# First LayerNorm's last eight tiles in two groups of four, transposed by TensorE, one mean-root product per group, and a new order of the whole program

## The chip, the core and the metric

The kernel runs on one core of one Trainium2 chip. Its time is device microseconds (us) of one execution, as the runs measure it; the profile is one such execution with every engine's instructions recorded. The engines are TensorE (PE in the profile; PEld is its weight load), VectorE (DVE), ScalarE (ACT), GpSimd (POOL) and SyncE (SP), which issues nearly all DMAs.

## What is computed

One transformer block on x of 2048 tokens by 512 features in bfloat16, with scales and shifts from a condition vector c:

```python
mod = (silu(c) @ w_mod).reshape(1, 6, 1, -1)           # sa, ca, ga, sb, cb, gb
h = layernorm(x) * (1 + ca) + sa
x = x + ga * A(h)                                      # linear attention
h = layernorm(x) * (1 + cb) + sb
x = x + gb * B(h)                                      # gated MLP, 512 -> 1376 -> 512

def A(h):                                              # 32 heads of 16
    q, k, v = split(h @ wqkv)
    phi(y) = [softmax(y @ w_phi), softmax(-y @ w_phi)] # 32 features a head
    num = phi(q) @ (phi(k)^T v);  den = phi(q) . sum(phi(k))
    return (num / den) @ wo

def B(h):
    return (sigmoid(h @ w_gate) * (h @ w_up)) @ w_down
```

## The kernel before

The 2048 tokens are 16 tiles of 128. The work is cut into some 900 named tasks; each is an instruction or a few on one engine. A text, ORDER, lists all their names in one sequence, written out by hand; `@A`, `@D` and `@P` after a name put it on ScalarE, VectorE or GpSimd where the task allows it, otherwise the first engine that it allows takes it. Each engine runs its own tasks strictly in that sequence, and so does the sync queue. Buffers (8 PSUM banks, 7 two-kilobyte slots for exponentials and features, and so on) are given out along the same sequence. Nothing is decided at run time.

The stages, each with the names used below:

- **Start.** Loads `ld_...`. TensorE transposes the key weight (`tpw`), ScalarE copies it (`wTc`), TensorE multiplies it by the block-diagonal w_phi (`fold`, whose operand `bd` GpSimd builds), ScalarE copies the result (`foldc`). `modc1` are one-column products that turn c into the first norm's scale and shift. `warm` are products on a zero tile whose results nobody reads.
- **First LayerNorm**, in the groups of tiles that LG lists. Per tile: statistics on VectorE (`st1`, lines 702 and 703). Per group: reciprocal root `rs1` (ScalarE by two activations, or GpSimd by two instructions, lines 712 and 713) and, on VectorE, minus mean times root (`nmr1`, line 718). Per tile: normalised tile `xn1` (line 731 on GpSimd). Then the transpose: by TensorE into a PSUM bank (`tph`, line 744; one task per group and 128 features), or, where TD is 1, by a transposing DMA on the sync queue (`xT1`, line 736). Then the scale and shift on the way to h1T (`hm1`, lines 751 and 753: the eviction of the transposes, or, after a DMA, a pass over h1T).
- **Keys and values**, per tile: products `K` (817) and `V` (821), exponentials `e` (776, ScalarE), sums `n` (780, VectorE), reciprocals `r`, features `phi` (787, GpSimd or VectorE), values with a column of ones `va`, and the accumulation `kv` (282) into two banks over all 16 tiles. Then `kvn` and `kvz` copy the sum (294, 299).
- **Queries**, per tile: `Q` (871), `qe`, `qn`, `qphi` (784) and a transposing DMA `pT`. Queries need only h1T, so their place in the order is free up to the use.
- **Attention output**, per tile, once the kv sum is there: numerators `num` (326), reciprocals `rd` (329), division `u` (333), a transpose (`tpo` and `oT` 347 for tiles 0 and 1, a DMA for the others), `out` (356), residual sum `x1` (361).
- **Second LayerNorm**: `st2`, `rs2`, `nmr2` (383), `xn2`, transpose `xnT`, modulation `mod` (422, 424, 426), for tile 0, tile 1, and then pairs.
- **MLP**, in six chunks of 1, 1, 2, 4, 4 and 4 tiles: gate and up products `g` and `u` (447, and 449 and 452 for the last 96 columns), `tg` (457), `hm` (468), and per tile the down products `y` (485), the final sum `fin` (492) and the store `st`. `tsw`, a table load on ScalarE (387), must stand between the last root taken there and the first `tg`. `wd` and `wo` scale the down and output weights.

Of the kernel before, what the change touches and what calls it, by code (L numbers as in the profile page):

```python
# [15 lines left out]
P = 128  # L16
# [14 lines left out]
LG = [[0], [1], [2, 3], [4, 5], [6, 7], [8, 9], [10, 11], [12, 13], [14, 15]]  # L31
TD = [0, 0, 0, 0, 0, 0, 1, 1, 0]
# [7 lines left out]
pmem ld_x0b wdz warm0 c1 warm1_0 warm1_1 bd st1_2 st1_3 warm1_2 warm1_3 c2 rs1_2 ld_x0a ld_wk0 warm1_4 tpw0 st1_0 rs1_0 wTc0 st1_1 ld_wk1 rs1_1 c3 xn1_0  # L40
nmr1_1 nmr1_2 ld_x1b st1_6 st1_7 tpw1 tpw3 wTc3 wTc1 tpw2 fold10 foldc10 wTc2 ld_wm00b ld_x1a ld_wm00a tph00 fold11 fold13 rs1_4 foldc13 fold12 foldc12 xn1_3
xn1_2 xn1_1 modc1.0 tph10 tph11 st1_4 tph20 tph01 ld_x2b foldc11 tph22 warm1_5 modc1c0 hm1_11@A nmr1_4 xn1_6 xn1_7 st1_5 rs1_3@P st1_11 st1_10 warm1_6
hm1_20@A hm1_10@A tph21 warm1_7 tph41 tph42 hm1_21 rs1_6@P nmr1_3 tph13 ld_wm01a ld_wm01b modc1.1 hm1_01@A hm1_00@A hm1_41@A tph03 tph23 K2a ld_x2a tph02
modc1c1 st1_8 ld_x3a warm1_8 K1a hm1_23 xn1_5 xn1_4 tph12 nmr1_6 st1_9 hm1_03@A hm1_13@A hm1_02@A ld_wv0 wqT3 xn1_10 xn1_11 rs1_5@P K0a K0b tph31 hm1_42@A
warm1_9 hm1_12@A hm1_22@A tph32 e0.0 K3a tph30 K3b hm1_30@A ld_wmga K1b tph33 warm1_10 tph40 st1_14 st1_15 st1_13 hm1_31@A hm1_32 wqT0 e3.0 wqT1 K2b hm1_40
nmr1_5 rs1_8@P n0.0 nmr1_8 hm1_33 e2.0 V0a V1a fold03 xn1_9 xn1_8 V1b V0b e1.0 n2.0 V2a V2b tph50 hm1_50 warm1_11 xn1_15 xn1_14 n1.0 V3a wqT2 fold00 fold01
tph43 r0.0@A va1 va0 phi0.0 foldc03 fold02 foldc01 foldc02 n3.0 st1_12 foldc00 xT1_10 xT1_11 r2.0 va2@D ld_wmm2 modca.0 modca.1 hm1_60@P hm1_63@P hm1_62@P
# [113 lines left out]
def kernel(  # L161
# [143 lines left out]
    def downstream(G):  # L305
# [7 lines left out]
        for p, tiles in enumerate(UNITS):  # L313
# [66 lines left out]
            if on_act:  # L380
                def f_nm(e, tiles=tiles):
                    for t in tiles:
                        dve.tensor_scalar(nmr[:, 1, t:t + 1], mv2[:, t, 0:1], rs2[:, t:t + 1], -1.0, op0=ALU.mult, op1=ALU.mult)
                G.add(f"nmr2_{p}", {"DVE": 0.07 * nt}, f_nm,
                      r=[("rs2", p)], w=[("nmr2", p)])
# [673 lines left out]
```

## Time and profile before

| what | us |
|---|---|
| median of 3 runs (lowest, highest) | 205.52 (204.65, 206.97) |
| the profiled execution's own time | 205.02 |
| its span, first to last instruction | 203.3 |
| TensorE busy | 194.9 (96%) |
| VectorE busy | 160.6 (79%) |
| ScalarE busy | 105.9 (52%) |
| GpSimd busy | 102.1 (50%) |
| DMA | 22.94 MB, mean 113 GB/s |

The granted TensorE clock was 1.0 over the span. Times on the trace count from the span's start; the 1.7 us between the span and the execution's own time lie around it. The ends of pipelined products are modelled, so a row's duration for TensorE is not what a product costs in a row of them: that is the distance from start to start. A few records of products are missing from the trace, which shows as a hole of exactly one product's length.

### The profile page before, as it was taken

What the parts mean: (1) busy time and instruction counts of PE and PEld (TensorE: products, weight loads), DVE (VectorE), ACT (ScalarE), POOL (GpSimd) and SP (SyncE); (2) the same over time, 40 slices, a digit from 0 to 9 for tenths busy, and PEclk for the clock granted to TensorE, in tenths of its full rate; (3) what the DMA queues carried; (4) which work ended last, traced back from release to release, by engine and by line L of the source; (5) the groups of instructions that cost most, each with busy time, mean ns of one, the idle gap of its engine ahead of it and who ended that gap; (6) DMA issues with size and microseconds to landing.
All of it is one profiled execution on the core that took longest, in us unless ns stands there. A gap on an engine that the chain in (4) does not pass through costs nothing.

```text
span 203.3 us, 4138 instructions
## 1 busy us (share of the span) xinstructions
PE 194.9 (96%) x1447; PEld 106.7 (52%) x1471; DVE 160.6 (79%) x374; ACT 105.9 (52%) x257; POOL 102.1 (50%) x143
## 2 busy tenths in 40 slices
PE   7789999999999999999999999999999999999993
PEld 2455655555464687668844444444444444444442
DVE  3899999999999999999897797794969844326633
ACT  2799999999978984556451115212113311324100
POOL 4698977789689999767670056230030324000000
PEclk9999999999999999999999999999999999999999
DMA  5999975669952792417637224433112030100111
GB/s 172 331 329 182 233 264 102 123 82 280 400 213 43 146 102 55 94 37 106 125 59 103 51 54 103 101 83 77 26 26 69 13 79 31 40 13 7 50 55 55
DMA packets 49453, 22.94 MB, mean 113 GB/s; under 512 B 38065, under 2 KB 47634, under 8 KB 49426
## 3 DMA queue, kind: packets, MB, share of 16 engines
q1 hardware_dynamic: 48896, 22.59, 48.6%
q8 instruction: 13, 0.21, 0.4%
q14 instruction: 14, 0.11, 0.2%
q10 hardware_dynamic: 530, 0.02, 0.1%
HBM read 11.58 MB, written 2.10 MB: 67 GB/s over the span
## 4 chain that ended last, share of the span: by engine, by line
PE 75%; DVE 8%; ACT 4%; DMA 4%; issue 4%; POOL 3%; SPq 0%; POOLq 0%; DVEq 0%
PE y_ps L485 19%; PE u_ps L447 18%; PE g_ps L447 17%; PE a_ps L356 5%; DMA wmod_sb<-in_w_mod_dram 4%; PE k_ps L817 3%; PE warm L600 3%; DVE ks L780 3%; PE num L326 2%; POOL phi L787 2%; PE q_ps L871 2%; PE v_ps L821 2%; PE g_ps L449 1%; ACT h1T L751 1%; DVE qks L780 1%
## 5 line engine op out<-in xcount | busy, mean ns | idle before, releaser
L457 ACT ACTIVATE tg<-g_ps 128x512 bf16<-128x512 f32 (+5 forms) x66 | 28.8, 455 | 66.7 <-PE g_ps L447 39.5
L468 DVE SCALAR_TENSOR_TENSOR wmod_sb<-tg,u_ps 128x512 bf16<-128x512 bf16 (+4 forms) x63 | 30.3, 492 | 18.0 <-ACT tg L457 11.3
L485 PE MATMUL y_ps<-wd_sb,wmod_sb 128*128 128x512 bf16 (+4 forms) x180 | 44.2, 366 | 0.2
L447 PEld LDWEIGHTS <-wg_sb 128*128 128x128 bf16 (+1 forms) x252 | 21.9, 99 | 16.1 <-issue 0.2
L447 PEld LDWEIGHTS <-wu_sb 128*128 128x128 bf16 (+1 forms) x252 | 21.8, 99 | 16.0 <-issue 0.3
L784 POOL TENSOR_TENSOR qphi<-qe,qks 128x512 bf16<-128x512 bf16 x24 | 25.1, 1063 | 3.9 <-DMA pT<-qphi 1.0
L485 PEld LDWEIGHTS <-wmod_sb 128*128 128x128 bf16 (+1 forms) x187 | 17.1, 98 | 16.0 <-issue 0.6
L447 PE MATMUL u_ps<-wT_sb,wu_sb 128*128 128x512 bf16 (+2 forms) x124 | 23.8, 322 | 0.1
L447 PE MATMUL g_ps<-wT_sb,wg_sb 128*128 128x512 bf16 (+2 forms) x122 | 23.0, 321 | 0.2
L447 PE MATMUL g_ps<-wqk_sb,wg_sb 128*128 128x128 bf16 (+4 forms) x127 | 19.9, 286 | 0.1
L447 PE MATMUL u_ps<-wqk_sb,wu_sb 128*128 128x128 bf16 (+4 forms) x127 | 19.8, 286 | 0.2
L492 DVE TENSOR_TENSOR ot<-y_ps,x 128x512 bf16<-128x512 f32 (+2 forms) x17 | 11.1, 654 | 10.5 <-PE y_ps L485 10.4
L780 DVE TENSOR_REDUCE qks<-qe 128x64 bf16<-128x1024 bf16 x16 | 19.2, 1204 | 0.0
L780 DVE TENSOR_REDUCE ks<-e 128x64 f32<-128x1024 bf16 (+2 forms) x22 | 19.1, 905 | 0.0
L376 POOL TENSOR_SCALAR ve<-mv 128x2 f32<-128x2 f32 (+1 forms) x8 | 1.8, 226 | 34.2 <-DVE mv L366 34.1
L776 ACT ACTIVATE e<-k_ps 128x512 bf16<-128x512 f32 (+2 forms) x44 | 17.7, 504 | 0.1
L776 ACT ACTIVATE qe<-q_ps 128x512 bf16<-128x512 f32 x32 | 17.3, 608 | 0.8 <-POOL phi L787 0.4
L787 POOL TENSOR_TENSOR phi<-e,kr 128x1024 bf16<-128x1024 bf16 (+2 forms) x10 | 14.5, 1454 | 3.9 <-ACT kr L795 2.1
L817 PE MATMUL k_ps<-wqk_f,h1T 128*128 128x512 bf16 x61 | 15.9, 379 | 0.1
L356 PE MATMUL a_ps<-wo_sb,oT 128*128 128x512 bf16 x60 | 15.9, 379 | 0.2
L871 PE MATMUL q_ps<-wqk_f,h1T 128*128 128x512 bf16 x60 | 15.7, 379 | 0.2
L821 PE MATMUL v_ps<-wv_sb,h1T 128*128 128x512 bf16 x62 | 15.5, 379 | 0.0
(131 smaller groups left out, 306.4 us busy)
## 6 DMA issues: line engine op xcount, KB each, us to landing
out_dram<-ot SPq DMA_DIRECT2D x15, 128.0 KB, 1.8
x_sb<-in_A_x_dram SPq DMA_DIRECT2D x6, 256.0 KB, 4.9
wmod_sb<-in_w_mod_dram SPq DMA_DIRECT2D x1, 1536.0 KB, 7.4
wu_sb<-in_B_w_up_dram SPq DMA_DIRECT2D x1, 1376.0 KB, 11.0
wg_sb<-in_B_w_gate_dram SPq DMA_DIRECT2D x1, 1376.0 KB, 10.4
wd_sb<-in_B_w_down_dram SPq DMA_DIRECT2D x1, 1280.0 KB, 8.0
wmod_sb<-in_w_mod_dram SPq DMA_DIRECT2D x4, 256.0 KB, 6.0
wqk_sb<-in_A_wqkv_dram SPq DMA_DIRECT2D x2, 256.0 KB, 4.5
```

Of the source, the lines that this page charges most:

```text
L356: pe.matmul(ap_[:], lhsT=oT[:, j, :], rhs=wo_sb[:, j, :], start=(j == 0), stop=(j == KT - 1))
L447: pe.matmul(ps[:fsz, 0:n], lhsT=w[:, j, ft * P:ft * P + fsz], rhs=h[:, j, 0:n], start=(j == 0), stop=(j == KT - 1))
L457: G.add(f"tg{k}.{ft}", {"ACT": 0.13 + n * 0.00083}, lambda e, tg=tg, g_ps=g_ps, fsz=fsz, n=n: act.activation(tg[:fsz, 0:n], g_ps[:fsz, 0:n ...
L468: dve.scalar_tensor_tensor(hm_all[:fsz, hm[k].slot, ft, 0:n], tg[:fsz, 0:n], 1.0, u_ps[:fsz, 0:n], op0=ALU.add, op1=ALU.mult)
L485: mm = pe.matmul(y[:, 0:c1 - c0], lhsT=hm_all[:fsz, hm[k].slot, ft, tl * P:(tl + 1) * P], rhs=wd_sb[:fsz, ft, c0:c1], start=(ft == 0), sto ...
L776: act.activation(ee[:, a:b, s].rearrange("p g f h -> p g (f h)"), kp[:, a * 64:b * 64].rearrange("p (g n) -> p g n", n=64), ACT.Exp, scale ...
L780: dve.tensor_reduce(ks[:, a:b].rearrange("p g s h -> p (g s) h"), ee[:, a:b].rearrange("p g s f h -> p (g s) h f"), axis=AX.X, op=ALU.add)
L784: engine(e).tensor_tensor(ph[:].rearrange("p (g s f h) -> p g s f h", s=2, f=DH, h=4)[:, :, s], ee[:, :, s], ks[:, :, 1 - s].unsqueeze(2). ...
L787: engine(e).tensor_tensor(ph[:, a * P:b * P].rearrange("p (g f h) -> p g f h", f=DH, h=4), ee[:, a:b].rearrange("p g s f h -> p (g s) f h" ...
L817: pe.matmul(kp[:], lhsT=h1T[:, j, t * P:(t + 1) * P], rhs=wqk_f[:, j, D:2 * D], start=(j == 0), stop=(j == KT - 1))
L821: pe.matmul(vp[:], lhsT=h1T[:, j, t * P:(t + 1) * P], rhs=wv_sb[:, j, :], start=(j == 0), stop=(j == KT - 1))
L871: pe.matmul(qp[:], lhsT=h1T[:, j, t * P:(t + 1) * P], rhs=wqk_f[:, j, 0:D], start=(j == 0), stop=(j == KT - 1))
```

## The change

LG has seven groups instead of nine: tiles 8 to 11 and 12 to 15 are one group each. TD is 0 everywhere, so tiles 10 to 13, which a DMA transposed, are transposed by TensorE too. A group of four fills a bank of 512 columns per 128 features, and one instruction evicts it. Minus mean times root is one instruction per group, in both norms. VectorE may normalise a tile of the first norm. ORDER is new throughout; its rows are not shown here, but as they fall on the engines.

```diff
-LG = [[0], [1], [2, 3], [4, 5], [6, 7], [8, 9], [10, 11], [12, 13], [14, 15]]
-TD = [0, 0, 0, 0, 0, 0, 1, 1, 0]
+LG = [[0], [1], [2, 3], [4, 5], [6, 7], [8, 9, 10, 11], [12, 13, 14, 15]]
+TD = [0, 0, 0, 0, 0, 0, 0]
 ORDER = """
-pmem ld_x0b wdz warm0 c1 warm1_0 warm1_1 bd st1_2 st1_3 warm1_2 warm1_3 c2 rs1_2 ld_x0a ld_wk0 warm1_4 tpw0 st1_0 rs1_0 wTc0 st1_1 ld_wk1 rs1_1 c3 xn1_0
+ld_x0b bd wdz warm0 c1 warm1_0 warm1_1 warm1_2 warm1_3 ld_x1b ld_wk1 ld_x0a c2 st1_3 st1_2 tpw2 tpw3 rs1_2 st1_7 nmr1_2 xn1_2@A wTc2 fold12 xn1_3 ld_wk0 tpw1
...
                 def f_nm(e, tiles=tiles):
-                    for t in tiles:
-                        dve.tensor_scalar(nmr[:, 1, t:t + 1], mv2[:, t, 0:1], rs2[:, t:t + 1], -1.0, op0=ALU.mult, op1=ALU.mult)
-                G.add(f"nmr2_{p}", {"DVE": 0.07 * nt}, f_nm,
+                    a, b = tiles[0], tiles[-1] + 1
+                    dve.scalar_tensor_tensor(nmr[:, 1, a:b], mv2[:, a:b, 0], -1.0, rs2[:, a:b], op0=ALU.mult, op1=ALU.mult)
+                G.add(f"nmr2_{p}", {"DVE": 0.2}, f_nm,
...
             def f_nm(e, ts=ts):
-                for t in ts:
-                    dve.tensor_scalar(nmr[:, 0, t:t + 1], mv1[:, t, 0:1], rs1[:, t:t + 1], -1.0, op0=ALU.mult, op1=ALU.mult)
-            G.add(f"nmr1_{g}", {"DVE": 0.02 + 0.1 * n}, f_nm,
+                a, b = ts[0], ts[-1] + 1
+                dve.scalar_tensor_tensor(nmr[:, 0, a:b], mv1[:, a:b, 0], -1.0, rs1[:, a:b], op0=ALU.mult, op1=ALU.mult)
+            G.add(f"nmr1_{g}", {"DVE": 0.2}, f_nm,
...
-            G.add(f"xn1_{t}", {"POOL": 0.69, "ACT": 0.73} if t else {"DVE": 0.3}, f_xn, ...
+            G.add(f"xn1_{t}", {"POOL": 0.69, "ACT": 0.73, "DVE": 0.4} if t else {"DVE": 0.3}, f_xn, ...
```

How the order falls on the engines at the three places that the prediction speaks of (line numbers after the change are one lower from the list of groups on).

GpSimd at the start, from the block-diagonal operand to the normalised tiles of the groups [2, 3] and [6, 7]. Before:

```order
L580 TENSOR_TENSOR bd_101<-wp_sb_100,bmask_76 128x4x64 x2
L731 TENSOR_SCALAR xn_245<-x_sb_65,rs1_84,nmr_89 128x512
L731 TENSOR_SCALAR xn_247<-x_sb_65,rs1_84,nmr_89 128x512
L731 TENSOR_SCALAR xn_249<-x_sb_65,rs1_84,nmr_89 128x512
L731 TENSOR_SCALAR xn_291<-x_sb_65,rs1_84,nmr_89 128x512
L731 TENSOR_SCALAR xn_293<-x_sb_65,rs1_84,nmr_89 128x512
```

Now, in the same place:

```order
L579 TENSOR_TENSOR bd_101<-wp_sb_100,bmask_76 128x4x64 x2
L730 TENSOR_SCALAR xn_184<-x_sb_65,rs1_84,nmr_89 128x512
L711 TENSOR_SCALAR ve1_83<-mv1_82 128x2
L712 TENSOR_TENSOR rs1_84<-ve1_83,mhalf_79 128x2
L711 TENSOR_SCALAR ve1_83<-mv1_82 128x1
L712 TENSOR_TENSOR rs1_84<-ve1_83,mhalf_79 128x1
L711 TENSOR_SCALAR ve1_83<-mv1_82 128x1
L712 TENSOR_TENSOR rs1_84<-ve1_83,mhalf_79 128x1
L730 TENSOR_SCALAR xn_242<-x_sb_65,rs1_84,nmr_89 128x512
L730 TENSOR_SCALAR xn_244<-x_sb_65,rs1_84,nmr_89 128x512
```

Three root pairs (of the groups [6, 7], [0] and [1]) have come from ScalarE to stand between the first normalised tile and the two of [6, 7]; the tiles 2 and 1 are normalised elsewhere.

VectorE from the copy of the kv sum's last part to the first residual sum (o is the divided output of a tile, den a reciprocal, qks a query sum). Before:

```order
L329 RECIPROCAL den_1233<-num_1208 128x16
L780 TENSOR_REDUCE qks_1240<-qe_1198 128x64
L333 TENSOR_TENSOR o_1242<-num_1183,den_1196 128x256
L329 RECIPROCAL den_1244<-num_1213 128x16
L329 RECIPROCAL den_1271<-num_1235 128x16
L333 TENSOR_TENSOR o_1242<-num_1213,den_1244 128x256
L333 TENSOR_TENSOR o_1231<-num_1235,den_1271 128x256
L361 TENSOR_TENSOR x1_1282<-a_ps_1261,x_sb_65 128x512
```

Now:

```order
L332 TENSOR_TENSOR o_1227<-num_1178,den_1183 128x256
L779 TENSOR_REDUCE qks_1237<-qe_1170 128x64
L332 TENSOR_TENSOR o_1239<-num_1187,den_1218 128x256
L328 RECIPROCAL den_1281<-num_1208 128x16
L360 TENSOR_TENSOR x1_1283<-a_ps_1241,x_sb_65 128x512
```

One division and one reciprocal of tile 1 have moved from ahead of the residual sum to behind it.

ScalarE from the second norm's first root to the modulations of tile 0 (oT is a copied transpose of an attention output). Before:

```order
L347 COPY oT_1304<-tpo_1299 128x512
L373 ACTIVATE ve2_87<-mv2_86,eps_96 128x1
L374 ACTIVATE rs2_88<-ve2_87 128x1
L400 ACTIVATE xn2_1333<-x1_1282,nmr_89,rs2_88 128x512
L387 ACT_TABLE_LOAD
L426 ACTIVATE wqk_sb_98<-tp_x_1344,modc_78 128x128 x2
```

Now:

```order
L372 ACTIVATE ve2_87<-mv2_86,eps_96 128x1
L373 ACTIVATE rs2_88<-ve2_87 128x1
L399 ACTIVATE xn2_1306<-x1_1283,nmr_89,rs2_88 128x512
L386 ACT_TABLE_LOAD
L346 COPY oT_1326<-tpo_1320 128x512
L425 ACTIVATE wqk_sb_98<-tp_x_1311,modc_78 128x128
L425 ACTIVATE wqk_sb_98<-tp_x_1310,modc_78 128x128
```

The copy of tile 1's attention output has moved from ahead of the root to behind the table load.

More of the change, by code (lines that the diff above doesn't have):

```diff
@@ L44 @@
[L44 to L47, printed above, removed]
```

89 lines of the change are left out of this document (46 added, 43 removed).

## The prediction

> **What bounds the kernel now.** I read the windows first, cut at TensorE's first key product, its first numerator product (just after the kv sum) and its first gate product. Columns: stretch, length, then busy time of PE, PEld, DVE, ACT and POOL.
>
> ```profile
> 14.20:58.02 43.82, 43.15 (x393) 24.02 (x397) 42.56 (x84) 42.36 (x117) 35.73 (x41) 1.00 0.90 220
> 58.57:68.89 10.32, 10.21 (x82) 5.52 (x85) 10.18 (x28) 8.67 (x18) 10.16 (x11) 1.00 0.36 73
> 68.89:200.10 131.21, 130.26 (x875) 71.14 (x888) 96.87 (x227) 44.91 (x98) 46.60 (x64) 1.00 0.33 63
> ```
>
> In the first stretch three engines are full at once: TensorE lacks 0.67 us, VectorE 1.3, ScalarE 1.5; only GpSimd has room (8 us). In the last one TensorE is alone at the limit. The idle time before its costliest group, 0.2 us in 174 products, says the same, and the end follows TensorE at a fixed distance:
>
> ```profile
> L485 PE MATMUL y_ps<-wd_sb,wmod_sb 128*128 128x512 bf16 (+4 forms) x174 | 43.9, 371 | 0.2
> 193.80 6.31 PE L485 MATMUL y_ps<-wd_sb,wmod_sb 128*128 128x512 bf16 x38
> 199.52 0.91 DVE L492 TENSOR_TENSOR ot<-y_ps,x 128x384 bf16<-128x384 f32 x2 [0.45 <-PE y_ps L485]
> ```
>
> So from the first gate product at 68.89 on, what counts is how much TensorE work is left when the first gate product starts. Before that it is a race of the engines to that start.
>
> Three spacings are needed:
>
> ```profile
> 62.40 1.02 PE L871 MATMUL q_ps<-wqk_f,h1T 128*128 128x512 bf16 x4
> 60.32 0.39 PE L345 MATMUL tpo<-ident,o 128*128 128x128 bf16 x4
> 28.90 0.82 PE L616 MATMUL modc_ps<-sc_bf,wmod_sb 128*128 128x1 bf16 x24 [0.22 <-DMA wmod_sb<-in_w_mod_dram]
> ```
>
> Four 512-column products take 1.02 us of which the last is 0.38, so they start 0.215 us apart; four transposes take 0.39 with a last one of 0.22, so 0.055 apart. 24 one-column products take 0.82 with a last one of 0.17, so 0.028 apart.
>
> **The change, part by part.**
>
> *Start to first key product.* In the new order GpSimd runs the operands of the folded weight, one normalised tile, three mean-root pairs (all three were ScalarE's) and two more normalised tiles before the transposes that TensorE has ahead of its first key product are fed.
>
> ```profile
> 5.24 1.50 POOL L580 TENSOR_TENSOR bd<-wp_sb,bmask 128x256 bf16<-128x256 bf16 x2 [2.13 <-DMA wp_sb<-in_A_w_phi_dram]
> 12.49 0.23 POOL L712 TENSOR_SCALAR ve<-mv 128x2 f32<-128x2 f32 x1
> 13.52 0.22 POOL L712 TENSOR_SCALAR ve<-mv 128x2 f32<-128x2 f32 x1
> 14.54 3.03 POOL L731 TENSOR_SCALAR xn<-x_sb,rs,nmr 128x512 bf16<-128x512 bf16 x4
> 14.20 0.38 PE L817 MATMUL k_ps<-wqk_f,h1T 128*128 128x512 bf16 x1
> ```
>
> The operands end at 6.74. A mean-root pair takes 13.52 - 12.49 = 1.03, a tile 3.03/4 = 0.76. So GpSimd is through at 6.74 + 0.76 + 3 x 1.03 + 2 x 0.76 = 12.11. TensorE then has nine transposes (0.50), 16 one-column products (0.45) and two hand-overs (about 0.1 each): first key product at about **13.25, 0.95 earlier**. ScalarE loses these three pairs and gains one normalisation, so it isn't later there. Half of the key weight still stands third in the sync queue, so TensorE's first weight transposes start as before.
>
> *First key product to first numerator.* TensorE's sum against before: the query product of tile 13 comes in (4 x 0.215 = +0.86); the first norm's tiles 10 to 13, which a DMA transposed, cost 16 transposes and two more fall behind the first key product (18 x 0.055 = +1.0); four warm-up products leave (-0.86) and two are put at the end, in the gap where the accumulated kv is copied (+0.43, hidden there). Without the hidden two: +1.0. The accumulation ends at 13.25 + 43.82 + 1.0 = **58.07** against 58.02.
>
> Does another engine end later? The rows that price this, grouped by shape (busy time, mean ns of one):
>
> ```profile
> 57.87 0.43 DVE L294 TENSOR_TENSOR kvb<-kvacc,mask 128x256 bf16<-128x256 f32 x1
> L751 ACT ACTIVATE h1T<-tp_h,modc 128x256 bf16<-128x256 bf16 x11 | 6.2, 587 | 0.0
> L753 POOL TENSOR_SCALAR h1T<-h1T,modc 128x256 bf16<-128x256 bf16 x7 | 3.9, 559 | 0.0
> L787 DVE TENSOR_TENSOR phi<-e,kr 128x1024 bf16<-128x1024 bf16 x7 | 4.7, 682 | 0.3 <-POOL h1T L753 0.3
> L787 POOL TENSOR_TENSOR phi<-e,kr 128x1024 bf16<-128x1024 bf16 x5 | 9.6, 1917 | 1.6 <-ACT kr L795 0.9 <-PE kvacc L282 0.5
> L753 DVE TENSOR_SCALAR h1T<-tp_h,modc 128x256 bf16<-128x256 bf16 x9 | 3.5, 393 | 0.6 <-PE tp_h L744 0.6
> L422 DVE TENSOR_SCALAR wqk_sb<-tp_x,modc 128x128 bf16<-128x128 bf16 x2 | 0.6, 340 | 0.0
> L729 DVE TENSOR_SCALAR xn<-x_sb,mv,rs 128x512 bf16<-128x512 bf16 x1 | 0.4, 404 | 0.0
> L718 DVE TENSOR_SCALAR nmr<-mv,rs 128x1 f32<-128x1 f32 x15 | 2.4, 203 | 0.3 <-ACT rs L710 0.3
> L299 DVE SCALAR_TENSOR_TENSOR kvb<-kvacc,mask 128x16 bf16<-128x16 f32 x2 | 0.3, 217 | 0.0
> L361 DVE TENSOR_TENSOR x<-a_ps,x_sb 128x512 f32<-128x512 f32 x16 | 10.8, 682 | 2.0 <-PE a_ps L356 1.8
> ```
>
> I took spacings from the timeline and counted each engine's instructions ahead of the copy of kv. VectorE: 16 evictions of transposes instead of 9, six of them 512 wide (+2.8); six more normalisations (+1.9); six fused mean-root products instead of 15 single ones (-1.0); eight feature products instead of twelve, the whole-tile ones going to GpSimd (-2.7); one query feature, one reciprocal and one value copy less, one modulation more (-1.0). Sum **0.0**: 53.0 us of work both times, ending at 57.87 if its waits stay as they were. ScalarE: eight evictions, one root group and more out, -2.4. GpSimd: four more whole-tile features at 1.92 (+8.6 with the parts), seven normalisations and seven evictions out (-5.3, -3.8), one more query feature (+1.0): +0.5 against 8 us of room. So TensorE stays the one that sets 58.07, with VectorE through 0.2 before it.
>
> Three prices have no row. A 512-wide eviction lies between the 256-wide one (393 ns, 0.32 apart) and the 512-wide float32 one (682, 0.61 apart); 128 to 256 columns adds 53 ns, so I take 0.46 apart. Six of them: -0.8 to +0.9. The fused product lies between one single product (0.13 apart) and the nearest fused form at its full 217 ns; I take 0.13, since it writes at most four columns: 0 to +0.5. A normalisation I take at 0.32 apart, at most its 404: 0 to +0.6. All three at the top make VectorE 2.0 longer, of which 0.2 is covered.
>
> The four removed transposing DMAs leave the sync queue, where they stood ahead of the large load that TensorE once waits for:
>
> ```profile
> 18.12 3.23 SPq L736 DMA_TRANSPOSE h1T<-xn  x2
> 21.41 0.57 SPq L556 DMA_DIRECT2D wmod_sb<-in_w_mod_dram  x1
> ```
>
> That load landed as TensorE's row at 28.90 began, with 0.22 of idle time. I leave the wait in; 0.22 is the bound of its gain.
>
> *First numerator to first gate product.* Here the chain is on VectorE and ScalarE.
>
> ```profile
> 65.30 0.20 ACT L374 ACTIVATE rs<-ve 128x1 f32<-128x1 f32 x1
> 65.67 0.20 DVE L383 TENSOR_SCALAR nmr<-mv,rs 128x1 f32<-128x1 f32 x1
> 65.79 0.75 DVE L333 TENSOR_TENSOR o<-num,den 128x256 bf16<-128x256 f32 x2
> 66.74 1.28 ACT L387 ACT_TABLE_LOAD   x1
> 64.48 0.59 ACT L347 COPY oT<-tpo 128x512 bf16<-128x512 bf16 x1
> 68.89 0.61 PE L447 MATMUL g_ps<-wqk_sb,wg_sb 128*128 128x128 bf16 x8
> ```
>
> Ahead of the first residual sum stand one reciprocal (0.17) and one division (0.35) fewer; one reciprocal leaves the place ahead of the statistics (0.15, what remains beside the shared start); the mean-root product no longer stands behind a 1.2 us query sum, which held it from 65.50 to 65.67 (0.17). Against that, the second attention output's copy now stands behind the table load and ahead of ScalarE's two modulations: +0.47. Net -0.37; with 0.05 from above the first gate product starts at **68.6**. TensorE has 9.6 us of work there by its instructions and the spacings above, five warm-ups (1.08) among it, where before two query products did useful work: those warm-ups fill idle time and cost nothing as long as this chain sets the start.
>
> *From there.* Query tile 10 is now left to do: 4 x 0.215 = **+0.86**; nothing else changes in sum. The nine mean-root products of the second norm and its transposes lie under TensorE.
>
> Sum: 0.05 - 0.37 + 0.86 = +0.54. The span goes from 203.3 to 203.8, and the profiled execution's own time from 205.02 to 205.6. The three runs shown have a median of 205.52, 0.5 above that execution; I put the prediction halfway, at **205.9**.
>
> **The rivals.** *The clock falls back.* TensorE has one warm-up less at the start, and one instead of three between its weight transposes and the first key product. Its start today:
>
> ```profile
> 1.24 2.74 PE L600 MATMUL warm<-wd_sb 128*128 128x512 bf16 x6 [1.24 <-DVE wd_sb L593]
> 6.24 1.36 PE L661 MATMUL tp_w<-ident,wqk_sb 128*128 128x128 bf16 x16
> ```
>
> The first six products are 0.43 apart against 0.215 later, and the 16 transposes take 1.36 where 0.055 apart would make 1.05, so half speed lasted to about 6.9. If the same 5.7 us (1.24 to 6.9) came again at 13.3, half of it would be lost: +2.85, **208.8**. Against it: no 512-column product stands between 6.2 and 12 us before either, and transposes at 13 us ran 0.055 apart. [...] Chance 0.10.
>
> *VectorE becomes the bound of the first long stretch.* If the wide evictions, the fused products and the normalisations all cost what their upper rows say, VectorE is 2.0 longer; it begins to tell at 0.2, and 1.8 goes into the end: **207.7**. For it: VectorE has no other room, and all four tiles of a group must be through before one eviction can start. Against it: all three bounds are needed at once. Chance 0.12.
>
> *The third chunk waits for GpSimd.* Its two last modulations stand behind the unit's root, three weight scalings and, new, two query features:
>
> ```profile
> 82.62 0.23 POOL L376 TENSOR_SCALAR ve<-mv 128x2 f32<-128x2 f32 x1 [1.34 <-DVE mv L366]
> 83.62 3.41 POOL L860 TENSOR_TENSOR wd_sb<-wd_sb,wmod_sb 128x512 bf16<-128x512 bf16 x3
> 88.75 1.10 POOL L424 TENSOR_SCALAR wqk_sb<-wqk_sb,modc 128x256 bf16<-128x256 bf16 x2 [1.72 <-PE g_ps L447]
> 89.82 1.06 POOL L784 TENSOR_TENSOR qphi<-qe,qks 128x512 bf16<-128x512 bf16 x1
> 89.90 0.60 PE L447 MATMUL g_ps<-wqk_sb,wg_sb 128*128 128x256 bf16 x4
> ```
>
> Today the modulations end at 89.85, and the chunk's first product starts at 89.90: there is no cover. With 2 x 1.06 more ahead of them, all of it paid: 205.9 + 2.1 = **208.0**. It decides if the root starts as late as 82.62 again; by the new order of VectorE its statistics stand 1.8 us of work earlier, and 1.72 of the wait before the modulations is for something else. Chance 0.10.
>
> *Faster.* The load's wait goes (0.22) and so does the rest of the 0.67 of idle time: 205.2, still within 1% of before. To be faster the first key product would have to come 2 us earlier as well, at 11.3, ahead of what GpSimd's rows allow: **203.2**. Chance 0.08.
>
> **How the numbers follow.** The forecast has 0.60, with a range of its own from 204.7 to 207.5. The 1% either way, which is about what a measurement of this kernel can tell from no change, lies at 203.5 and 207.6: faster 0.08, within 0.60, slower 0.10 + 0.12 + 0.10 = 0.32. The range runs from 204.3 (205.2 less the 0.9 by which the lowest run shown lies under the median) to 208.8, which takes in the three slower rivals; the faster one is left out.
>
> **What would show it.** Right: first key product near 13.3, first numerator near 58.6, first gate product near 68.6, TensorE idle under 1.5 us after it, VectorE within 0.5 us of TensorE at the copy of kv. Wrong: key products 0.43 apart at 13 us (clock); a VectorE that starts copying kv after 59 with no wait on TensorE; a gap ahead of the second or third chunk's gate products; a first key product before 12.

## The result and the profile after

The changed kernel takes 212.22 us (median of four runs, 211.08 to 212.38) against 205.22 for the kernel before: 1.032 times as long, 95% interval 1.026 to 1.038. The prediction was 205.9, with a range to 208.8. The profiled execution took 211.08, with a span of 209.3 against 203.3.

Cut at the first key product, the first numerator product, the first product of the first chunk and the end of the last output product, the windows of the changed kernel are these. (The prediction's first window ended with the accumulation, at 58.02; the table counts to the first numerator, at 58.57 before.) Columns: stretch, length, then busy time of PE, PEld, DVE, ACT and POOL, and the granted clock.

```profile
12.99:60.84 47.85, 45.19 (x421) 25.31 (x419) 47.14 (x88) 43.11 (x118) 36.36 (x34) 1.00 0.73 207
60.84:71.39 10.55, 10.37 (x83) 5.19 (x82) 10.45 (x28) 7.71 (x15) 9.08 (x10) 1.00 0.41 76
71.39:205.40 134.01, 132.75 (x894) 71.63 (x892) 97.60 (x224) 46.66 (x101) 45.36 (x60) 1.00 0.30 62
```

| stretch, us | before | predicted | changed |
|---|---|---|---|
| start to first key product | 14.20 | 13.25 | 12.99 |
| to first numerator | 44.37 | 45.35 | 47.85 |
| to first chunk's first product | 10.32 | 10.0 | 10.55 |
| to the end of the last output product | 131.21 | 132.1 | 134.01 |
| to the end of the span | 3.2 | 3.2 | 3.9 |

TensorE's own work grew as forecast. By row spacings it is 190.8 us against 189.9, so of the 6.0 us between the spans 0.9 is work, 0.7 lies behind the last output product and the rest is idle time. Those last 0.7 are not shown to be the change's: over the profiled executions of all versions this tail was 3.1 to 3.9 us, and 3.8 in e6, which has the order of the kernel before. Who is waited for stands in the list of TensorE's waits: a normalisation on VectorE (line 728) and a hidden tile on VectorE (line 467), neither of which stood in that list before. Columns: waiting instruction, what it waited for, total us, times, longest.

```profile
PE tp_h L743 <- DVE xn L728: 2.6, 3, 1.4
PE u_ps L446 <- DVE wmod_sb L467: 0.9, 1, 0.9
```

The timeline of the changed kernel shows why VectorE is late. Columns: start, us, engine, line, operation, tiles, count, and in brackets the idle time of the engine before it.

```profile
20.62 1.91 POOL L786 TENSOR_TENSOR phi<-e,kr 128x1024 bf16<-128x1024 bf16 x1
20.66 2.03 DVE L728 TENSOR_SCALAR xn<-x_sb,mv,rs 128x512 bf16<-128x512 bf16 x1
23.43 0.29 PE L743 MATMUL tp_h<-ident,xn 128*128 128x128 bf16 x2 [1.05 <-DVE xn L728]
34.87 3.24 DVE L728 TENSOR_SCALAR xn<-x_sb,mv,rs 128x512 bf16<-128x512 bf16 x3
36.04 1.92 POOL L786 TENSOR_TENSOR phi<-e,kr 128x1024 bf16<-128x1024 bf16 x1 [0.32 <-ACT kr L794]
38.17 0.34 PE L743 MATMUL tp_h<-ident,xn 128*128 128x128 bf16 x3 [1.35 <-DVE xn L728]
65.63 2.07 POOL L783 TENSOR_TENSOR qphi<-qe,qks 128x512 bf16<-128x512 bf16 x2
67.13 0.58 DVE L382 SCALAR_TENSOR_TENSOR nmr<-mv,rs 128x1 f32<-128x1 f32 x1
85.26 2.28 POOL L859 TENSOR_TENSOR wd_sb<-wd_sb,wmod_sb 128x512 bf16<-128x512 bf16 x2
85.67 0.76 DVE L382 SCALAR_TENSOR_TENSOR nmr<-mv,rs 128x2 f32<-128x2 f32 x1
86.47 1.35 DVE L397 TENSOR_SCALAR xn<-x,rs,nmr 128x512 bf16<-128x512 f32 x1
88.07 0.61 PE L446 MATMUL u_ps<-wT_sb,wu_sb 128*128 128x128 bf16 x8 [0.87 <-DVE wmod_sb L467]
```

A normalisation that the prediction put at 0.32 lasts 2.03, and it ends 0.15 after the GpSimd product that had started just before it (20.62 + 1.91 = 22.53 against 22.69). The second group's three take 3.24 and end 0.15 after another one. The fused products at 67.13 and 85.67 end with a GpSimd instruction too (67.70, 86.4), and the second norm's normalisation at 86.47 ends 0.3 after one (87.5). Not every overlap is a wait: another normalisation took 0.41 at 9.55, while GpSimd was at a root of 128x1 from 9.43 to 10.0. Before, the single product at 65.67 took 0.20 in the middle of a GpSimd query feature.

### The profile page after: what moved, and what is told of

It is laid out like the page before. It is cut to its first block, busy times and chain, and to the rows that moved or that the text cites. A ratio compares the mean times of both kernels' runs of the same rounds, so it can differ in the third digit from the quotient of the medians.

```text
span 209.3 us, 4155 instructions
## 1 busy us (share of the span) xinstructions
PE 197.3 (94%) x1487; PEld 107.2 (51%) x1487; DVE 164.8 (79%) x368; ACT 105.7 (50%) x249; POOL 99.8 (48%) x129
## 4 chain that ended last, share of the span: by engine, by line
PE 64%; DVE 7%; issue 1%; ACT 0%; DVEq 0%
PE y_ps L484 18%; PE g_ps L446 17%; PE u_ps L446 16%; PE a_ps L355 6%; PE q_ps L870 2%; PE num L325 2%; DVE qks L779 1%; PE g_ps L448 1%; DVE phi L786 1%; DVE wmod_sb L467 1%; PE u_ps L451 1%; PE warm L599 1%; DVE x L360 1%; DVE st L364 1%; DVE o L332 0%
## 5 line engine op out<-in xcount | busy, mean ns | idle before, releaser
L456 ACT ACTIVATE tg<-g_ps 128x512 bf16<-128x512 f32 (+4 forms) x66 | 28.8, 455 | 70.9 <-PE g_ps L446 43.4
L484 PE MATMUL y_ps<-wd_sb,wmod_sb 128*128 128x512 bf16 (+4 forms) x187 | 46.1, 367 | 0.1
L467 DVE SCALAR_TENSOR_TENSOR wmod_sb<-tg,u_ps 128x512 bf16<-128x512 bf16 (+4 forms) x63 | 29.6, 489 | 17.2 <-ACT tg L456 10.2
L783 POOL TENSOR_TENSOR qphi<-qe,qks 128x512 bf16<-128x512 bf16 x27 | 28.0, 1055 | 12.6 <-DVE qphi L783 7.3
L786 POOL TENSOR_TENSOR phi<-e,kr 128x1024 bf16<-128x1024 bf16 (+2 forms) x14 | 23.0, 1649 | 5.7 <-ACT vaug L835 2.7
L446 PE MATMUL g_ps<-wT_sb,wg_sb 128*128 128x512 bf16 (+2 forms) x124 | 23.8, 322 | 0.2 <-ACT wT_sb L425 0.2
L446 PE MATMUL g_ps<-wqk_sb,wg_sb 128*128 128x256 bf16 (+4 forms) x128 | 19.8, 287 | 0.0
L816 PE MATMUL k_ps<-wqk_f,h1T 128*128 128x512 bf16 x64 | 16.5, 379 | 0.0
```

What stands on the lines that cost most here:

```text
L446: pe.matmul(ps[:fsz, 0:n], lhsT=w[:, j, ft * P:ft * P + fsz], rhs=h[:, j, 0:n], start=(j == 0), stop=(j == KT - 1))
L456: G.add(f"tg{k}.{ft}", {"ACT": 0.13 + n * 0.00083}, lambda e, tg=tg, g_ps=g_ps, fsz=fsz, n=n: act.activation(tg[:fsz, 0:n], g_ps[:fsz, 0:n ...
L467: dve.scalar_tensor_tensor(hm_all[:fsz, hm[k].slot, ft, 0:n], tg[:fsz, 0:n], 1.0, u_ps[:fsz, 0:n], op0=ALU.add, op1=ALU.mult)
L484: mm = pe.matmul(y[:, 0:c1 - c0], lhsT=hm_all[:fsz, hm[k].slot, ft, tl * P:(tl + 1) * P], rhs=wd_sb[:fsz, ft, c0:c1], start=(ft == 0), sto ...
L783: engine(e).tensor_tensor(ph[:].rearrange("p (g s f h) -> p g s f h", s=2, f=DH, h=4)[:, :, s], ee[:, :, s], ks[:, :, 1 - s].unsqueeze(2). ...
L786: engine(e).tensor_tensor(ph[:, a * P:b * P].rearrange("p (g f h) -> p g f h", f=DH, h=4), ee[:, a:b].rearrange("p g s f h -> p (g s) f h" ...
```

## The experiments

Two theories. **Lock**, the author's name for what the rows above suggest (a normalisation of 2.03 us that ends 0.15 after a GpSimd product, against 0.41 for the one at 9.55): VectorE's bf16 normalisation and its fused product, both new here, end only when the GpSimd instruction beside them has ended. **Load**: VectorE simply has too much to do, or a group of four needs its tiles too early. A third cause, the **clock**, came up with the first runs, and the medians given below include it. The versions ran on three chips, each beside the kernel before, whose medians there were 206.24 (e1 to e4), 205.14 (e5 to e8) and 205.63 (e9 to e11); each ratio is against those runs.

**e1: the prices by themselves.** The kernel issues, in each part, four each of
```
xn : tensor_scalar(xn, x, mean, root, subtract, mult)            # new normalisation
xa : the same with accum_out=ac                                  # it writes an accumulator too
nmf: scalar_tensor_tensor(nmr[:, 0:4], mean, -1.0, root, mult, mult)  # fused product
nmt: tensor_scalar(nmr[:, t:t+1], mean, root, -1.0, mult, mult)  # single product
```


> Computes nothing of the reference: it only measures VectorE forms, four times each, with a 1.2 us sum between any two, first while GpSimd is idle, then while GpSimd runs 128x1024 two-input products without a pause, then 512-wide normalisations, then memsets. Lock theory: the bf16 normalisation and the fused mean-root product take 0.35 and 0.15 us while GpSimd is idle, and end only when GpSimd's running instruction ends, so up to 1.9 us more, behind the products; the single mean-root product, an eviction from PSUM, and a normalisation that also writes an accumulator take the same in all parts. Rival (these forms are slow by themselves, or their operands were late): the same times in all parts, with none over 0.8 us.

Rows of its tiles, grouped; durations are min/median/max in ns, then first and last start. GpSimd is idle in the first row of each pair and runs 1.9 us products in the second.

```profile
L96 DVE TENSOR_SCALAR xn<-x_sb,mv,rs x4: 400/402/404, 8.6 to 12.9; 128x512 bf16<-128x512 bf16 x4
L96 DVE TENSOR_SCALAR xn<-x_sb,mv,rs x4: 865/866/950, 55.8 to 61.7; 128x512 bf16<-128x512 bf16 x4
...
L97 DVE TENSOR_SCALAR_CACHE_REDUCE xa<-x_sb,mv,rs x4: 792/792/793, 14.4 to 19.9; 128x512 bf16<-128x512 bf16 x4
L97 DVE TENSOR_SCALAR_CACHE_REDUCE xa<-x_sb,mv,rs x4: 792/792/792, 63.6 to 69.2; 128x512 bf16<-128x512 bf16 x4
...
L99 DVE SCALAR_TENSOR_TENSOR nmf<-mv,rs x4: 151/152/152, 28.1 to 31.9; 128x4 f32<-128x4 f32 x4
L99 DVE SCALAR_TENSOR_TENSOR nmf<-mv,rs x4: 733/816/818, 79.3 to 84.8; 128x4 f32<-128x4 f32 x4
...
L100 DVE TENSOR_SCALAR nmt<-mv,rs x4: 203/204/205, 33.1 to 36.9; 128x1 f32<-128x1 f32 x4
L100 DVE TENSOR_SCALAR nmt<-mv,rs x4: 196/204/204, 86.7 to 90.4; 128x1 f32<-128x1 f32 x4
```

The normalisation took 0.40 us where GpSimd rested and 0.87 beside the products, the fused product 0.15 and 0.82. The single product (0.20) and the accumulator's form (0.79) took the same in both parts, and so did an eviction from PSUM (0.80). Two forms that the kernel before has too took longer in some parts: VectorE's feature product 0.68 alone and 2.04 for the first of its four beside the products, and the second norm's normalisation with its float32 input between 0.53 and 1.06 over its sixteen. The normalisation's extra was 0.46 to 0.55 here, each time behind a 1.2 us sum, and some 1.6 in the changed kernel, where the one of 2.03 began 0.04 after GpSimd's product. That the wait follows from where in GpSimd's instruction it begins is the author's reading; e1 did not vary it. So the fused product was 0.05 us cheaper than one single product where GpSimd rested, and 0.6 dearer beside these products.

**e2: the form that took 0.79 us in both parts of e1.** It writes an accumulator besides, and the seven tiles' normalised values come out otherwise, so its time is used and not its output.
```diff
-  dve.tensor_scalar(xn, x_sb, mv1, rs1, op0=subtract, op1=mult)
+  dve.tensor_scalar(xn, x_sb, mv1, rs1, op0=subtract, op1=mult, accum_out=accs)
```


> The changed kernel, with VectorE's seven normalisations of the first norm writing an accumulator too (which nobody reads). Lock theory: each is about 0.3 us longer by itself (0.6 to 0.7), but waits for no GpSimd instruction; TensorE's gaps of 1.2 us at 22 and 1.5 us at 37 shrink to 0.3 or less each, and the time falls from 212.2 to about 210. Rival (VectorE has too much work, or a group of four needs its four tiles too early): the longer normalisations make the gaps longer by 0.3 and 0.9 us, about 213.4.

210.97 us; 1.026 (1.019 to 1.032) of before, an interval that overlaps the changed kernel's. Its trace decides. The form takes 0.80, more than assumed, and runs in the middle of GpSimd's product:

```profile
21.27 3.79 POOL L787 TENSOR_TENSOR phi<-e,kr 128x1024 bf16<-128x1024 bf16 x2
21.30 0.80 DVE L729 TENSOR_SCALAR_CACHE_REDUCE xn<-x_sb,mv,rs 128x512 bf16<-128x512 bf16 x1
```

The window of its first long stretch:

```profile
13.63:59.70 46.07, 45.18 (x421) 25.29 (x419) 45.36 (x93) 43.14 (x118) 36.37 (x34) 1.00 0.73 211
```

The first long stretch falls from 47.85 to 46.07, and TensorE's gaps ahead of the transposes of the two groups of four fall from 1.2 and 1.5 us to 0.4 and 0.55. Seven instructions that are twice as long by themselves made the stretch 1.8 us shorter: that speaks for the lock and against load. The numerator itself comes 1.14 earlier (59.70 against 60.84), because the first key product comes 0.64 later behind one of the slower normalisations; of the 1.8 us between the two spans another 0.5 lies in the tail.

**e3: five normalisations on ScalarE.**
```diff
-  xn1_10@D  xn1_11@D  xn1_12@D  xn1_13@D  xn1_14@D
+  xn1_10@A  xn1_11@A  xn1_12@A  xn1_13@A  xn1_14@A
```


> The changed kernel, with the five later normalisations of the first norm (tiles 10, 11, 12, 13, 14) on ScalarE in place of VectorE, in the same places of the order. Lock theory: VectorE gets 5.7 us back (three that took 2.03, 1.00 and 2.00 and two of 0.31 and 0.40), TensorE's two gaps of 2.7 us together go, 3.6 us of work on ScalarE takes back up to 1 us of it: 209.5 to 210.5. Rival (grouping by four, whoever normalises): the gaps stay, since four tiles must be ready before a transposed group: within 0.5 of 212.2.

213.0 us; 1.034 (1.025 to 1.042). Neither number came. VectorE's normalisations no longer stand in TensorE's list of waits, but ScalarE is now the late one:

```profile
PE tp_h L743 <- ACT xn L726: 2.0, 2, 1.4
PE v_ps L820 <- ACT e L775: 1.2, 1, 1.2
```

ScalarE was the third full engine of that stretch; 3.6 us more did not fit. It tells nothing between the theories, since it replaces one late engine by another.

**e4: the second norm as before.**
```diff
-  dve.scalar_tensor_tensor(nmr[:, 1, a:b], mv2[:, a:b, 0], -1.0, rs2[:, a:b], ...)
+  for t in tiles: dve.tensor_scalar(nmr[:, 1, t:t+1], mv2[:, t, 0:1], rs2[:, t:t+1], -1.0, ...)
-  xn2_3@D
+  xn2_3@A
```


> The changed kernel, with the second norm alone as before: one mean-root product per tile again, and the normalisation of tile 3 on ScalarE in place of VectorE. Lock theory: the product ahead of the first gate product took 0.58 in place of 0.16 us, the one before tile 3 took 0.76, and tile 3's normalisation 1.35 in place of 0.54; TensorE's wait of 1.0 us at 87 goes, and the first gate product comes 0.4 us earlier against the numerator: 210.7 to 211.2. Rival (those waits are covered by TensorE's other work, the second norm costs nothing): within 0.3 of 212.2.

210.93 us; 1.023 (1.016 to 1.029), 1.3 us under the changed kernel. TensorE's wait at 87 is gone. So the second norm, which the prediction had called hidden, cost some 1.0 to 1.3 us. Its trace also showed something else, which the changed kernel's one profile lacks:

```profile
9.00:13.00 4.00, 2.77 (x51) 1.88 (x50) 3.61 (x13) 3.31 (x9) 3.67 (x7) 1.00 1.26 269
13.00:16.70 3.70, 3.70 (x27) 2.01 (x24) 2.79 (x10) 2.73 (x8) 1.74 (x3) 0.56 1.51 251
```

The windows have the granted clock third from the end; the timeline has this row of two key products:

```profile
13.38 1.01 PE L816 MATMUL k_ps<-wqk_f,h1T 128*128 128x512 bf16 x2
```

From 13.4 to 16.8 the granted clock is half (0.56 over the second window, which takes in the last of the full speed), and the key products are 0.43 apart. Three of the changed kernel's four runs have the mean clock that goes with it (0.992) and take 212.1 to 212.4; the profiled one (0.999) took 211.08.

**e5: without the forms that had waited.** Five normalisations on GpSimd, the second norm as in e4.
```diff
-  xn1_10@D  xn1_11@D  xn1_12@D  xn1_13@D  xn1_14@D
+  xn1_10    xn1_11    xn1_12    xn1_13    xn1_14      # GpSimd
```


> The changed kernel without the forms that waited: the five later normalisations of the first norm on GpSimd in place of VectorE, one mean-root product per tile in the second norm, and tile 3's second normalisation on ScalarE. Lock theory: TensorE's waits of 1.2 us at 22, 1.5 us at 37 and 1.0 us at 87 go, and 0.4 us ahead of the first gate product; GpSimd takes 3.8 us more, out of 11 that it has idle in that stretch, which may cost up to 1 us again: 208.0 to 209.5. Rival (a group of four needs its tiles too early, whoever normalises; the run with ScalarE had 3.2 us of such waits): only the second norm's part is gained, 210.5 to 211.2.

209.48 us; 1.023 (1.017 to 1.029), at the edge of the lock theory's range, but not for its reasons alone: the first long stretch is 47.72, hardly better than 47.85. Part of its 2.7 us under the changed kernel is the clock: three of its four runs had 0.998 or more. TensorE's wait at 22 is gone, and in place of the others it waits for GpSimd's features and normalisations and a value copy of ScalarE (two of TensorE's waits, then a window of it):

```profile
PE kvacc L281 <- ACT vaug L835: 0.7, 1, 0.7
PE kvacc L281 <- POOL phi L786: 0.7, 2, 0.4
```

```profile
18.00:56.60 38.60, 36.58 (x329) 20.08 (x334) 34.99 (x58) 34.57 (x96) 36.37 (x35) 1.00 0.69 211
```

GpSimd is busy 36.4 of 38.6 us there. The 11 us of room that the expectation counted on lay at the ends of the stretch.

**e6: the kernel before, with fused products alone.**
```diff
-  for t in tiles: dve.tensor_scalar(nmr[:, t:t+1], mv[:, t, 0:1], rs[:, t:t+1], -1.0, ...)
+  dve.scalar_tensor_tensor(nmr[:, a:b], mv[:, a:b, 0], -1.0, rs[:, a:b], ...)
```


> The kernel before, with the fused mean-root products alone. Lock theory: the product ahead of the first gate product stood at 65.67 while GpSimd's query feature ran from 65.17 to 66.22; fused it ends with that feature, 0.35 us later, and the first gate product with it: 0.2 to 0.6 us slower than before in the span (203.3), and single ones of the nine of the second norm take 0.4 to 0.8 in place of 0.2. Rival (the fused form only saves work): all of them under 0.25 us, and up to 0.5 us faster.

206.62 us; 1.0065 (1.0034 to 1.0096). An edit that issues fewer instructions makes the kernel 1.3 us slower, more than twice the most that was expected: besides the product ahead of the first gate product, one that had been thought hidden waited longest and held up TensorE.

```profile
65.53 0.56 DVE L383 SCALAR_TENSOR_TENSOR nmr<-mv,rs 128x1 f32<-128x1 f32 x1
83.75 3.40 POOL L860 TENSOR_TENSOR wd_sb<-wd_sb,wmod_sb 128x512 bf16<-128x512 bf16 x3
83.81 1.11 DVE L383 SCALAR_TENSOR_TENSOR nmr<-mv,rs 128x2 f32<-128x2 f32 x1 [0.17 <-POOL rs L377]
85.17 0.38 PE L447 MATMUL g_ps<-wT_sb,wg_sb 128*128 128x128 bf16 x4 [0.53 <-DVE wmod_sb L468]
```

**e7: the kernel before, with four normalisations on VectorE.**
```diff
-  xn1_15    xn1_14    ...  xn1_12    xn1_13
+  xn1_15@D  xn1_14@D  ...  xn1_12@D  xn1_13@D
```


> The kernel before, with four of the first norm's normalisations (tiles 12 to 15) on VectorE in place of GpSimd, in their places of the order. Lock theory: those that meet a GpSimd instruction take up to 1.9 us more than 0.35, two or three of the four do, VectorE (1.3 us of room in that stretch) gets 3 to 5 us more, and the numerator comes 1 to 3 us later: 206.2 to 208.5. Rival (0.35 each, GpSimd relieved by 3 us): within 0.7 of before.

207.11 us; 1.011 (1.005 to 1.016). The numerator came 1.2 us later (59.74). One of the four met a GpSimd product, not two or three; the pair with it took 2.03, the other pair 0.72 (at 29.86):

```profile
22.07 1.92 POOL L787 TENSOR_TENSOR phi<-e,kr 128x1024 bf16<-128x1024 bf16 x1 [1.00 <-ACT kr L795]
22.43 2.03 DVE L729 TENSOR_SCALAR xn<-x_sb,mv,rs 128x512 bf16<-128x512 bf16 x2
```

**e8: the changed kernel, with four warm-ups back at the start.**
```diff
-  tpw2 tpw3 ... foldc10 tph03 ... tph00 tph41
+  tpw2 tpw3 warm warm ... foldc10 warm tph03 ... tph00 tph41 warm
```


> The changed kernel, with four of the seven moved warm-up products back at the start (two after the second weight transpose, one ahead of the first, one ahead of the third product for the scale). Clock theory: in most runs of the changed kernel the granted clock is 0.992 on average, in the records a half-speed stretch from 13.2 to 16.8, which costs 1.2 to 1.7 us; with these four the stretch before it is busier, the clock stays at 0.999 to 1.000 in most runs, and the median falls by about 1 us to 211.1. Rival (the clock falls back at random, or for what lies ahead of 6 us): as many runs at 0.992 as before, 212.2, or 0.3 more for products that delay others.

211.03 us (210.68 to 211.33); 1.028 (1.024 to 1.031). The four stood behind the kv sum (two) and between the first numerator and the first chunk (two). All six runs have a mean clock of 0.998 or more, against one of four of the changed kernel, and the median is 1.2 us lower. In the profile the clock holds:

```profile
9.00:13.00 4.00, 3.31 (x52) 2.12 (x52) 3.61 (x13) 3.20 (x9) 3.66 (x7) 1.00 1.21 274
13.00:16.70 3.70, 3.65 (x38) 2.23 (x36) 3.63 (x12) 3.70 (x10) 1.76 (x3) 1.00 1.50 250
```

That the warm-ups held it is not shown by this run alone, since the chips differ. On its chip the kernel before kept 0.998 or more in 11 of 17 runs and e5, without these warm-ups, in three of four; on the chip of e2 to e4 the kernel before kept it in one of seven, and those three versions, without these warm-ups, in two of twelve. Nor does the share of busy time decide it: of the 5 us before 13 TensorE was busy 4.1 here and 3.5 in e4, but 3.2 in the profile of the kernel before, which held, and 4.1 in e3's, which fell back. The price of the dip doesn't hang on that: the changed kernel's own runs at 0.992 are 1.0 to 1.3 us above its run at 0.999.

The two warm-ups taken out between the first numerator and the first chunk (0.43 of work) changed that stretch by 0.1: they had filled idle time.

**e9: e2, e4 and e8 together.**

> The changed kernel with three edits at once: the accumulator form for VectorE's first-norm normalisations, the second norm as before (one mean-root product per tile, tile 3 on ScalarE), and the four warm-ups back at the start. The single edits gained 1.25, 1.3 and 1.2 us. If lock waits (two places) and the clock are separate causes they add up: 212.2 - 3.7 = 208.5, all runs with a clock of 0.998 or more, no wait of TensorE on a normalisation over 0.8 us. If they are one cause, seen three times (a later start of the same chain): 210 to 211. What is left above before is then 0.9 us of TensorE work for the transposes and some 2 us that neither theory names.

208.51 us; 1.014 (1.007 to 1.021), where the sum of the single gains gave 208.5. Three of the four runs had a clock of 0.999 or more. Medians hold a mix of clocks, so the check is better made at full clock: the changed kernel's 211.08, less 1.8 (e2's profiled execution against it) and 1.0 (e4's one run at 1.0), is 208.3, and e9's three runs have 208.2 to 208.6. So the gains of the two lock edits add up, as those of separate causes do. Its windows:

```profile
13.94:60.11 46.17, 44.87 (x419) 25.18 (x417) 45.46 (x93) 43.24 (x118) 36.39 (x34) 1.00 0.72 208
60.11:70.29 10.18, 10.04 (x79) 4.91 (x80) 10.07 (x28) 7.68 (x15) 8.97 (x10) 1.00 0.39 78
70.29:203.15 132.86, 132.48 (x894) 71.66 (x892) 96.75 (x230) 47.14 (x102) 45.33 (x60) 1.00 0.30 63
```

**e10: the kernel before, with TensorE transposes for tiles 10 to 13.**
```diff
-TD = [0, 0, 0, 0, 0, 0, 1, 1, 0]
+TD = [0, 0, 0, 0, 0, 0, 0, 0, 0]
-  xT1_10 xT1_11 ... hm1_60@P hm1_63@P hm1_62@P ...
+  tph60 hm1_60 tph63 hm1_63 tph62 hm1_62@A ...
```


> The kernel before, with tiles 10 to 13 of the first norm transposed by TensorE in place of the DMA, in pairs as its other tiles, each transposed block ahead of its eviction, evictions shared by VectorE and ScalarE in place of GpSimd. TensorE theory: 16 transposes at 0.055 are 0.9 us of work in a stage that it fills: 206.0. Rival (the evictions decide: VectorE and ScalarE have 1.3 and 1.5 us of room there, and get 1.3 and 1.9 us more): 206.5 to 207.5. Rival (TensorE had 0.67 us idle there, which the transposes fill, and the sync queue is rid of four transfers): 205.0 to 205.4.

211.47 us; 1.029 (1.022 to 1.036): far above all three expectations. TensorE's work grew by the 0.9 us, its idle time by 2.7 ahead of the first numerator, by 0.7 more until the first chunk was under way and by 0.4 after. VectorE and ScalarE took over eight evictions (the second rival, whose 1.3 and 1.9 us of work were too small a price; the run doesn't part the evictions from the transposes), and with the moved times a feature product of VectorE (0.68 alone in e1) now takes 1.09 beside GpSimd's normalisations (a window, then the timeline):

```profile
13.90:62.17 48.27, 45.83 (x417) 25.33 (x415) 45.30 (x91) 44.17 (x121) 32.19 (x34) 1.00 0.71 196
```

```profile
28.82 1.52 POOL L731 TENSOR_SCALAR xn<-x_sb,rs,nmr 128x512 bf16<-128x512 bf16 x2 [2.01 <-DVE nmr L718]
29.78 1.09 DVE L787 TENSOR_TENSOR phi<-e,kr 128x1024 bf16<-128x1024 bf16 x1 [1.02 <-PE kvacc L282]
```

So in an order that was not made for them the transposes and their evictions cost 4.9 us between the profiled spans (208.2 against 203.3), and 5.8 in the medians, in which the clock has a part (0.981 and 0.984 in two of the four runs). The changed kernel's new order brings that down: with the lock waits out (e9), TensorE's idle time up to the numerator, 8.9 us by row spacings, is only 0.4 above the kernel before.

**e11: the kernel before, with three warm-ups moved to 7.8 and 9.0 us.**
```diff
-  ... warm1_9 ... warm1_10 ... warm1_11 ...
+  ... tph00 warm warm fold11 fold13 warm ...
```


> The kernel before, with its last three warm-ups (at 14.8, 16.7 and about 25 us) moved to 7.8 and 9.0 us, where TensorE waits for ScalarE. Clock theory: some runs of the kernel before have a half-speed stretch from 11.3 to 14.6 (mean clock 0.983 to 0.992) and take up to 2 us more; with a busier 7 to 10 us nearly all runs have 0.998 or more, and 0.4 us of warm-ups is gone from a full stage: a median of 204.6 to 204.9, faster than both kernels. Rival (the clock falls back for something else): as many runs under 0.995 as before, 205.1.

204.86 us against 205.63 for the kernel before on the same chip: 0.9962 (0.9927 to 0.9997). Ten of its twelve runs have a clock of 0.998 or more; of the seventeen of the kernel before beside them, five. Here both ran side by side on one chip, so this is the run that shows what warm-ups do for the clock. They are not all of the gain: among the runs at 0.998 or more alone the medians are 204.7 and 205.2. It is the fastest of all these versions, and the only one under both kernels, by 0.4%.

## Why the prediction was wrong, step by step

**Start: right in its time, with some luck.** First key product at 12.99, forecast 13.25. GpSimd was through at 11.52, not 12.11: it came to its first tile 0.3 earlier, and a root for one tile took 0.88, not the 1.03 of a pair. From there to the key product it took 1.47 and not 1.14, for TensorE's last transposes then waited for a normalisation of VectorE (until 11.94), which the forecast chain didn't have. The two hand-overs of 0.1 in that chain stand in no row; here a transpose began 0.05 to 0.06 after the normalisation of VectorE that it waited for (11.94 to 12.00, 23.38 to 23.43, 38.11 to 38.17).

**First stretch: the step "a normalisation I take at 0.32 apart, at most its 404" failed.** The bounds came from rows of these forms without asking what GpSimd did at that moment. The one normalisation of the profile before (404 ns, at 7.25) ran between two GpSimd instructions that ended at 6.74 and began at 8.57. Here one lasted 2.03 beside a GpSimd product of 1.91. Three of seven paid it, 4.0 us of VectorE time together against the 0.6 allowed, and 1.8 us of the stretch (47.85 to 46.07 in e2). The fused product's 0.13 to 0.217 held here (0.15 and 0.16 in this stretch) and failed in the second norm (0.58, 0.46 and 0.76), and the wide eviction was priced right (0.43 to 0.46 apart). The term for TensorE's work, +1.0, was right: e9 has 46.17 where 45.35 was forecast, and the waits of 0.4 and 0.55 on its slower normalisations are about that difference.

e1 has the prices form by form, alone and beside GpSimd's products: 0.40 and 0.87 for the normalisation, 0.15 and 0.82 for the fused product, 0.79 both times for the normalisation with an accumulator. The first two are forms that the diff adds, and for neither did the prediction ask what it costs beside GpSimd.

**The rival "VectorE becomes the bound"** named the engine and the place, not the mechanism: its price was the sum of the upper rows (1.8), and its instructions were not long (0.40 alone in e1) but kept waiting (2.03). 0.12 was too little for it, since the same rows that bounded it from above did not show its worst case.

**First numerator to first gate product: the sign failed.** Forecast -0.3, measured +0.23. Two steps did it; the 0.84 us that the forecast took off the chain ahead of them did come. First, the fused product: ScalarE's normalisation behind it starts 6.91 us after the first numerator, where the forecast's terms make 6.50 (7.34 before, less 0.84). In e4, with single ones, it is 6.54. Second, what follows the table load. From its end to the first chunk the forecast had 1.34 (0.87 before, and 0.47 for the copy), and it took 1.53. In the new order TensorE's output product of tile 1 stands ahead of the first chunk; it needs that copy and takes 0.86, and the forecast had no term for it.

```profile
68.58 1.28 ACT L386 ACT_TABLE_LOAD   x1
69.87 0.58 ACT L346 COPY oT<-tpo 128x512 bf16<-128x512 bf16 x1
70.51 1.04 PE L355 MATMUL a_ps<-wo_sb,oT 128*128 128x512 bf16 x4
71.17 0.46 ACT L425 ACTIVATE wqk_sb<-tp_x,modc 128x128 bf16<-128x128 bf16 x1 [0.35 <-DVE wqk_sb L421]
71.39 0.56 PE L446 MATMUL u_ps<-wqk_sb,wu_sb 128*96 128x128 bf16 x4
```

0.41 and 0.19 make the 0.60 between 10.55 and the 9.95 of the forecast's chain. ScalarE's second modulation is late as well, by 0.35, since VectorE's stands behind a query sum; the third of the chunk's first four products begins 0.18 later for it. No run moves the output product.

**From there: "nothing else changes in sum" failed.** Forecast +0.86, measured +2.8. The mean-root product of tiles 2 and 3 (0.76) and tile 3's normalisation (1.35) stand ahead of hidden tiles that TensorE needs; e4 took 1.0 us of idle time away. In e9 the stretch is still 1.65 longer than before, of which 0.86 is query tile 10. The other 0.8 us is idle time in a few gaps between 80 and 91 us, from the second chunk's first gate products (0.5, of which the list gives 0.2 to ScalarE's modulation) onward; no run takes it away.

**The clock rival happened,** with a chance of 0.10, and beside the others: half speed for 3.4 us in e4's profile, not the 5.7 that its +2.85 was worked out from. Over its first key products e4's TensorE lost 1.7 us by row spacings; in the time it is 1.2 (212.22 to 211.03 in e8). In the runs beside e11 the kernel before had a mean clock of 0.992 or less in 12 of 17, so its median of 205.2 may already hold some of it.

**The third chunk's rival** did not show: no wait of its gate products stands in TensorE's list.

The sum, then: 1.3 (second norm), 1.2 (clock) and 1.3 to 1.8 (first norm's lock waits) of the 7.0 are each taken away by an edit, and together in e9 3.7. Some 3 us remain. Between the profiled spans it is 3.3 (206.6 against 203.3), where the forecast had 0.5. The other 2.8 are, by stretch: 0.7 ahead of the first key product, where e9 has its warm-ups back and a gap of 0.7 behind one of its own slower normalisations; 0.8 in the first long stretch, with gaps of 0.4 and 0.55 behind two more of them; 0.2 up to the first chunk; 0.8 in the gaps after 80 us; and 0.3 in the tail. The gaps after 80 us are located, not explained.

## What to carry over

When an edit puts a new form of instruction on VectorE, look up what GpSimd runs at that moment before taking a price from a row: the normalisation that took 0.40 us alone took 0.87 beside e1's products and 2.03 beside one in the changed kernel, and e6, with fewer instructions, was 1.3 us slower. Bound such a price by the GpSimd instructions near it (1.91 there), not by the same form's longest row (0.404); behind back-to-back ones, as in e1, it came to 7.62. When an instruction moves, look also at what waits for it on the other engines and how long that takes. Try warm-up products where TensorE is idle at the start: with three of them at 7.8 and 9.0 us, ten of e11's twelve runs had a clock of 0.998 or more, against five of the seventeen beside them. And a median over runs may hold a clock dip that the one profile does not show, as in the changed kernel's runs (0.992 in three of four, the profiled one 0.999).

## What was not expected of the hardware

In e1, behind one hundred GpSimd memsets without a pause, VectorE's normalisation did not get a turn between two of them but at their end:

```profile
268.66 89.52 POOL L91 MEMSET gms<- 128x1024 bf16 x100
270.02 88.31 DVE L96 TENSOR_SCALAR xn<-x_sb,mv,rs 128x512 bf16<-128x512 bf16 x1
```

The first one behind back-to-back GpSimd normalisations of 0.77 took 7.62, the length of nine or ten of them; the median of the four there was 0.49 and the shortest 0.44.

The clock's dip was as long in each of the three profiles that show one. Worked out from the granted clock of windows of one microsecond, it goes from 13.6 to 17.0 us in e3, from 13.4 to 16.8 in e4 and from 11.5 to 14.9 in e6, 3.4 us each time. The half speed at the start ends at different times. The kernel before has it to about 6.9 by the prediction's rows. The four warm-ups at 4.11 take 1.05 in the changed kernel and 1.89 in e4, and e4's eight transposes at 6.11 take 0.83 where 0.055 apart would make 0.61: full speed from about 4.2 in the one and 6.6 in the other, estimated from these rows. The granted clock reads 1.00 in all of these stretches, so the kernel before's clock of 1.0 does not cover its start. That a dip meets other instructions in each run, and that this is why one kernel has it in some runs only, is the author's guess, not shown.
